# Matmuls on the identity ahead of TensorE's steps in the first job of a fused attention and mixture-of-experts kernel

## The chip, the cores and the metric

The kernel runs on one core of a Trainium2 chip. The metric is the device time of one execution in microseconds (us). The time before is 248.84 us, the median of three runs (248.19 to 251.78).

The engines are named as in the profile: PE is TensorE's matmul and PEld its weight load, DVE is VectorE, ACT is ScalarE, POOL is GpSimd, SP is SyncE, which issues the transfers here.

## The reference: what is computed

Attention with a sliding window and sink positions, over 4 batches, 8 heads, 768 positions and 64 columns per head, and on its output a soft mixture of 8 experts with 4 slots each. All is float32.

```python
scores = scale * np.matmul(q, k.transpose(0, 1, 3, 2))
keep = is_sink | in_window            # first 4 positions, or the last 128 up to the own one
a = exp(scores - max) / (sum + 1e-09) # where keep, else 0
x = (a @ v) in rows of 512, one per token

logits = x @ phi                      # 32 slots
d = softmax of logits over the tokens;  slot_input = d.T @ x
slot_out[e] = relu(slot_input[e] @ w1[e]) @ w2[e]
out = softmax of logits over the slots @ slot_out
```

## The kernel before, in words

The attention is cut into 12 jobs (line 690): a job is one batch b and 256 query positions j. A job loads q, k and v of its positions (load, line 712), transposes k and q (prep, 729), makes four tiles of scores and their softmax (softmax, 765: two quads of heads, each with the even and the odd 64 rows of every block of 128), transposes the weights of a quad (weights_transposed, 841) and the weights of the sink positions (sinks_transposed, 851), masks the transposed weights (select, 863) and multiplies with v (values, 875). Then the tokens go through the gate of the mixture (Moe.tokens, 307). After the twelfth job the experts' weights, two matrices of 16 MB together 32 transfers of 1 MB, are multiplied (Moe.tail, 511). In the first job, prep works in two halves, and the four sink rows of v are split into a high and a low part (sink_values, 74).

No loop sets the order of the work. Each piece is a step with an engine, an estimated time, what it reads and writes, and a key (Plan.add, 161). Plan.order (167) runs a list schedule over all steps with these estimates: it takes the step that could start first, and the smallest key among those. Plan.issue (251) then writes the instructions in the order of the planned starts, each engine's queue being in order. At a TensorE step it takes the step's bank or banks of PSUM (lines 258 to 260): "s" is the pool of two score tiles of two banks each, "w" the pool of four single banks for all the rest. A new tile's first writer waits until the last reader of the tile that had the bank before has finished.

The kernel has matmuls on the identity already: 8 before the plan starts (line 1158), 10 steps of 128 columns that the plan puts where TensorE is free at the start (busy, line 925, with a key of 1000), and up to 64 of 64 columns in the last job (line 964). Nothing reads what they write.

The names in the profile: first is the buffer of loaded q and k, wt any of a pool of large slots (the transposed k, the weights, v, the experts' weights), qt the transposed q, s and w the PSUM tiles, pst and vsink the transposed sink weights and the sink rows of v, ident the identity. All instructions that the plan issues have line 127, that of the helper which records them.

Of the kernel before, what the change touches and what calls it, by code (L numbers as in the profile page):

```python
# [19 lines left out]
P = 128  # L20
# [96 lines left out]
class Engine:  # L117


    def __init__(self, tc, engine):  # L120
        self.tc, self.engine = tc, engine
# [19 lines left out]
class Plan:  # L141
# [8 lines left out]

    IDLE = 900.0

    def __init__(self, pools):

        self.pools, self.steps, self.modes, self.handles = pools, [], [], 0
# [95 lines left out]
    def issue(self):  # L251
        order = sorted(self.order())
        end = max(t for t, _, i, e in order if e == "P" and self.steps[i][0] < self.IDLE)
        for t, _, i, e in order:
            _, _, _, fn, _, _, new, _ = self.steps[i]
            if t > end and self.steps[i][0] >= self.IDLE:
                continue
            for x in new:
                pool, shape, _ = self.pools[x["kind"]]
                x["tile"] = pool.tile(shape, F32, name=x["kind"])  # L260
            fn(e)


# [384 lines left out]
def window_path(ctx, tc, c, moe, q, k, v, phi, w1, w2, out):  # L648
# [6 lines left out]
    nc = moe.nc = Core(tc)  # L655
    B, H, S, D = q.shape
    NJ = S // 256
    plan = Plan(moe.pools)
# [5 lines left out]
    def slot():  # L664
        return slots.tile([P, 2048], F32, name="wt")

    t, u = moe.first
# [7 lines left out]
    t = slot()  # L675
# [3 lines left out]
    t = slot()  # L679
# [245 lines left out]
    def busy(e, h, n=P):  # L925
        nc.tensor.matmul(h["tile"][:, 0:n], lhsT=c.ident, rhs=c.ident[:, 0:n], start=True, stop=True)


    for _ in range(WARM[1]):
        h = plan.psum()  # L930
# [196 lines left out]
def fused(ctx, tc, q, k, v, n_sink, window, phi, w1, w2, out):  # L1127
# [42 lines left out]
    with tc.If(flag == 1) as cmp:  # L1170
        with ExitStack() as c2:
            window_rest(tc, moe, *window_path(c2, tc, c, moe, q, k, v, phi, w1, w2, out), out)
# [33 lines left out]
```

## Time and profile before

| | |
|---|---|
| median of three runs | 248.84 us |
| profiled execution | 248.67 us |
| its span (first to last instruction) | 247.0 us |
| mean granted clock of TensorE | 0.971 |
| busy share of PE, DVE, ACT, POOL | 87%, 65%, 61%, 57% |
| mean DMA rate over the span | 241 GB/s |
| instructions | 8602, of them 3356 matmuls on PE |

How to read it: the profile's slices cut the span into 40 equal parts and give busy time in tenths, the clock that TensorE was granted in tenths of full speed, and the share of the 16 DMA engines in use. The chain is the work that ended last, followed back from the end. In the timeline a row is a group of like instructions, with the start in us from the span's begin, the time, and in brackets the engine's idle time ahead of it and what ended it. In a table of windows stand the window, its length, the busy time of PE, PEld, DVE, ACT and POOL with their instructions in brackets, the granted clock, the DMA share and GB/s.

### The profile page before, as it was taken

How to read it: one execution, taken by the hardware profiler on the slowest of the kernel's cores; microseconds unless marked ns; L12 is line 12 of the kernel's file. 1: busy time of each engine (PE TensorE's matmuls, PEld its weight loads, DVE VectorE, ACT ScalarE, POOL GpSimd, SP SyncE). 2: the span in 40 equal slices, each digit the busy share in tenths (PEclk: the TensorE clock that was granted, in tenths of full speed). 3: DMA queues.
4: the chain of work that ended last, by engine and by line, in shares of the span. 5: the costliest groups of instructions: out<-in, count | busy, mean ns of one | idle time of the engine just before them, and what ended most of it. 6: DMA issues, size and time to landing. Idle time of an engine off the chain costs nothing.

```text
span 247.0 us, 8602 instructions
## 1 busy us (share of the span) xinstructions
PE 214.8 (87%) x3356; PEld 152.0 (62%) x3356; DVE 161.3 (65%) x440; ACT 151.1 (61%) x577; POOL 141.9 (57%) x281
## 2 busy tenths in 40 slices
PE   7953899898999799999979899997999999999820
PEld 7733566576777567776747677664787534556520
DVE  4289568759899956889994888997544611225340
ACT  2167569869778886968888686888643411214320
POOL 2036687976857995885789497678995141000000
PEclk9996799999999999999999999999999999999985
DMA  5597989999899799999999999460149989999896
GB/s 117 114 199 157 169 255 280 257 268 287 240 213 285 239 284 262 281 251 205 265 202 245 242 335 198 91 215 1 31 160 330 372 333 344 348 349 367 315 319 204
DMA packets 102963, 59.44 MB, mean 241 GB/s; under 512 B 76292, under 2 KB 98820, under 8 KB 102916
## 3 DMA queue, kind: packets, MB, share of 16 engines
q1 hardware_dynamic: 102916, 58.83, 86.0%
q8 instruction: 28, 0.46, 0.8%
q14 instruction: 19, 0.16, 0.2%
HBM read 52.53 MB, written 6.29 MB: 238 GB/s over the span
## 4 chain that ended last, share of the span: by engine, by line
PE 51%; DVE 28%; ACT 13%; issue 4%; POOL 0%; ACTq 0%; DVEq 0%; POOLq 0%
PE w L127 34%; PE s L127 15%; DVE wt L127 13%; ACT wt L127 9%; DVE s L127 9%; DVE rs L127 2%; PE w L1158 2%; DVE first L127 1%; ACT wt L582 1%; ACT first L127 1%; DVE call L127 1%; DVE acc L127 1%; DVE sums L127 0%; DVE wt L567 0%; DVE vsink L127 0%
## 5 line engine op out<-in xcount | busy, mean ns | idle before, releaser
L127 ACT ACTIVATE wt<-s,wt 128x132 f32<-128x132 f32 x192 | 68.5, 376 | 10.7 <-DVE wt L127 4.5
L127 POOL TENSOR_TENSOR wt<-wt 128x528 f32<-128x528 f32 x96 | 63.8, 670 | 19.4 <-DVE wt L127 8.2
L127 POOL TENSOR_SCALAR_AFFINE_SELECT wt<-wt 128x512 f32<-128x512 f32 x88 | 54.4, 640 | 15.6 <-DVE sums L127 9.8
L127 PE MATMUL w<-wt 128*64 128x128 f32 (+3 forms) x550 | 50.7, 317 | 1.6 <-DVE wt L567 1.0
L127 PE MATMUL s<-wt,qt 64*64 64x196 f32 (+2 forms) x768 | 43.1, 332 | 10.0 <-ACT wt L127 7.0
L127 PEld LDWEIGHTS w<-wt 128*64 128x64 f32 (+2 forms) x550 | 35.9, 140 | 13.8 <-DVE wt L567 2.1
L127 ACT ACTIVATION_READ_ACCUMULATOR wt<-s,wt 128x1 f32 x192 | 40.5, 211 | 0.0
L127 PEld LDWEIGHTS s<-wt,qt 64*64 64x64 f32 x768 | 27.0, 136 | 20.1 <-ACT wt L127 10.5
L127 DVE TENSOR_REDUCE wt<-s 128x4 f32<-128x528 f32 x48 | 33.9, 707 | 1.7
L127 PE MATMUL w<-ident,wt 64*128 64x64 f32 (+1 forms) x442 | 28.9, 239 | 3.7 <-POOL wt L127 1.2
L127 ACT COPY wt<-w 128x512 f32<-128x512 f32 (+1 forms) x41 | 23.7, 581 | 11.7 <-PE w L127 8.6
L127 PEld LDWEIGHTS w<-ident,wt 64*128 64x128 f32 (+1 forms) x442 | 21.2, 142 | 13.2 <-issue 6.6
L127 DVE COPY wt<-w 128x512 f32<-128x512 f32 (+1 forms) x33 | 22.0, 666 | 10.8 <-PE w L127 10.8
L127 PEld LDWEIGHTS w<-ident,first 64*128 64x128 f32 x576 | 21.8, 141 | 10.7 <-issue 5.0
L127 PE MATMUL w<-ident,first 64*128 64x64 f32 x576 | 26.9, 231 | 1.5 <-ACT first L127 1.5
L127 ACT COPY first<-w 128x512 f32<-128x512 f32 x32 | 18.6, 592 | 15.5 <-PE w L127 15.4
L127 DVE COPY_PREDICATED s<-later,s 128x256 f32<-128x256 uint8 x48 | 20.4, 425 | 4.4 <-PE s L127 3.2
L127 DVE TENSOR_TENSOR wt<-wt 128x4 f32<-128x4 f32 x48 | 13.6, 283 | 10.2 <-ACT wt L127 9.0
L127 ACT ACTIVATE qt<-w 128x512 f32<-128x512 f32 (+1 forms) x25 | 14.4, 579 | 6.2 <-PE w L127 4.3
L127 PE MATMUL s<-wt 128*32 128x256 f32 x256 | 14.4, 380 | 0.0
L127 PE MATMUL w<-wt,si 128*32 128x512 f32 x112 | 14.1, 594 | 0.0
L127 POOL COPY wt<-wt 128x512 f32<-128x512 f32 (+2 forms) x13 | 5.7, 455 | 13.5 <-ACT wt L127 11.0
(115 smaller groups left out, 246.1 us busy)
## 6 DMA issues: line engine op xcount, KB each, us to landing
wt<-in_moe_w_dram SPq DMA_DIRECT2D x30, 1024.0 KB, 8.2
wt<-in_v_dram SPq DMA_DIRECT2D x24, 256.0 KB, 4.5
first<-in_q_dram SPq DMA_DIRECT2D x22, 256.0 KB, 5.5
first<-in_k_dram SPq DMA_DIRECT2D x22, 256.0 KB, 4.6
out_dram<-wt SPq DMA_DIRECT2D x4, 1024.0 KB, 7.6
first<-in_moe_w_dram SPq DMA_DIRECT2D x2, 1024.0 KB, 5.1
out_dram<-wt SPq DMA_DIRECT2D x3, 512.0 KB
first<-in_k_dram SPq DMA_DIRECT2D x4, 128.0 KB, 2.3
```

The lines of the kernel that those rows point to most:

```text
L127: return self.tc.keep_in_program_order(f(*args, **kw))
L582: (nc.vector.tensor_copy if n % 2 else nc.scalar.copy)(ob[:, 2 * (n - n0):2 * (n - n0) + 2], yp)
L1158: nc.tensor.matmul(t[:, 0:P], lhsT=c.ident, rhs=c.ident, start=True, stop=True)
```

## The change

Plan.issue gets a variable, free, the planned end of the last TensorE step. When a TensorE step is planned to start later than that, and its planned start is below 30 us, the gap divided by 0.11 us gives a number of matmuls, which are issued right ahead of the step into the step's own (first) bank. Each multiplies the 128x128 identity with 64 of its columns. The step's own first matmul starts a new accumulation and overwrites what they wrote. The order of the steps stays the same, and the other engines' instructions do too.

```diff
+    FILL = 30.0
...
     def issue(self):
         order = sorted(self.order())
         end = max(t for t, _, i, e in order if e == "P" and self.steps[i][0] < self.IDLE)
+        free = None
         for t, _, i, e in order:
...
             for x in new:
                 pool, shape, _ = self.pools[x["kind"]]
                 x["tile"] = pool.tile(shape, F32, name=x["kind"])
+            if e == "P":
+                if free is not None and t < self.FILL:
+
+                    for _ in range(int((t - free) / 0.11)):
+                        self.fill(new[0]["tile"])
+                free = t + self.steps[i][2][0]
             fn(e)
...
+    def fill(t):
+        nc.tensor.matmul(t[:, 0:64] if len(t.shape) == 2 else t[:, 0, 0:64], lhsT=c.ident, rhs=c.ident[:, 0:64],
+                         start=True, stop=True, skip_group_check=True)
+
+    plan.fill = fill
```

99 such matmuls are issued, called fills below, ahead of 16 steps: 1, 1 and 3 among the first transposes and identity matmuls, 8 ahead of the first scores, 1 ahead of the second half of the transposes, 19 ahead of the sink rows' matmul, 1 and 3 ahead of the first job's other scores, 2 ahead of the second job's transposes of q, 19 ahead of the first transposes of weights, 3 ahead of the second job's transposes of k, 20 ahead of its scores, 1 ahead of the next transposes, 15 ahead of the sink transposes, 1 ahead of the next scores and 1 ahead of the first values. Three of these places follow, as the instructions stand on TensorE; the brackets are the semaphores that an instruction waits for.

The sink rows' matmul (w<-wt 128x256), behind the transposes of q and k of the first job. Before:

```order
L127 MATMUL w<-ident,first_76 128x64 [waits DMAHW0_49]
L127 MATMUL w<-ident,first_76 128x64 x3
L127 MATMUL w<-wt 128x256 [waits DMAHW6_49,DMAHW5_49,DMAHW7_49,DMAHW4_49,Activation_49]
L127 MATMUL s<-wt,qt 64x68 [waits DVE_49,Activation_49,Pool_49]
L127 MATMUL s<-wt,qt 64x196 [waits DVE_49]
```

Now:

```order
L127 MATMUL w<-ident,first_76 128x64 [waits DMAHW0_49]
L127 MATMUL w<-ident,first_76 128x64 x3
L127 MATMUL w<-ident 128x64 [waits Activation_49]
L127 MATMUL w<-ident 128x64 x18
L127 MATMUL w<-wt 128x256 [waits DMAHW6_49,DMAHW7_49,DMAHW5_49,DMAHW4_49]
L127 MATMUL s<-ident 128x64 [waits DVE_49,Activation_49]
L127 MATMUL s<-wt,qt 64x68 [waits Pool_49]
L127 MATMUL s<-wt,qt 64x196 [waits DVE_49]
```

The wait for ScalarE, which frees the bank, has gone from the step to the first of its 19 fills.

The second job's first scores (s<-wt,qt 64x196), behind its transposes of k. Before:

```order
L127 MATMUL w<-ident,first_76 128x64 [waits DMAHW3_49]
L127 MATMUL w<-ident,first_76 128x64 x7
L127 MATMUL s<-wt,qt 64x196 [waits DVE_49]
L127 MATMUL s<-wt,qt 64x196 [waits Activation_49]
L127 MATMUL s<-wt,qt 64x196 x14
```

Now:

```order
L127 MATMUL w<-ident,first_76 128x64 [waits DMAHW3_49]
L127 MATMUL w<-ident,first_76 128x64 x7
L127 MATMUL s<-ident 128x64 x20
L127 MATMUL s<-wt,qt 64x196 [waits DVE_49]
L127 MATMUL s<-wt,qt 64x196 [waits Activation_49]
L127 MATMUL s<-wt,qt 64x196 x14
```

Here the 20 fills wait for nothing, and the step still waits for VectorE, which copies the transposed k.

The sink transposes (w<-ident,wt 128x128), behind the second transposes of weights (w<-ident,wt 128x64). Before:

```order
L127 MATMUL w<-ident,wt 128x64 [waits Pool_49]
L127 MATMUL w<-ident,wt 128x64 x7
L127 MATMUL w<-ident,wt 128x128 [waits Activation_49]
L127 MATMUL w<-ident,wt 128x128 [waits Pool_49]
L127 MATMUL s<-wt,qt 64x196 [waits DVE_49]
```

Now:

```order
L127 MATMUL w<-ident,wt 128x64 [waits Pool_49]
L127 MATMUL w<-ident,wt 128x64 x7
L127 MATMUL w<-ident 128x64 [waits Activation_49]
L127 MATMUL w<-ident 128x64 x14
L127 MATMUL w<-ident,wt 128x128
L127 MATMUL w<-ident,wt 128x128 [waits Pool_49]
L127 MATMUL s<-ident 128x64 [waits DVE_49]
```

Again the wait for ScalarE, for the bank, has gone from the step to the first of 15 fills.

## The prediction

> **What bounds the kernel now.** I read the page first: the span, the slices of busy time and the chain that ended last.
>
> ```profile
> span 247.0 us, 8602 instructions
> ...
> PE   7953899898999799999979899997999999999820
> ...
> PEclk9996799999999999999999999999999999999985
> DMA  5597989999899799999999999460149989999896
> ...
> PE w L127 34%; PE s L127 15%; DVE wt L127 13%; ACT wt L127 9%; DVE s L127 9%; DVE rs L127 2%; PE w L1158 2%; DVE first L127 1%; ACT wt L582 1%; ACT first L127 1%; DVE call L127 1%; DVE acc L127 1%; DVE sums L127 0%; DVE wt L567 0%; DVE vsink L127 0%
> ```
>
> A slice is 6.2 us. TensorE is at 9 or 8 in nearly all of them and holds half of the chain (51% in the page's sum by engine). It is idle mainly in the first five slices, the ones that the change fills, and the fourth and fifth are the only ones before the very end in which its granted clock is below full. The windows place that dip:
>
> ```profile
> 20.00:22.00 2.00, 1.29 (x23) 1.27 (x24) 1.85 (x7) 1.85 (x8) 1.12 (x3) 0.71 0.79 174
> 22.00:24.00 2.00, 0.37 (x7) 0.18 (x3) 2.00 (x4) 1.37 (x8) 1.84 (x2) 0.50 0.33 75
> 26.00:28.00 2.00, 2.00 (x30) 1.20 (x24) 1.17 (x3) 0.00 (x0) 1.38 (x4) 0.58 1.23 209
> 28.00:30.00 2.00, 1.04 (x32) 0.90 (x30) 1.93 (x5) 1.98 (x10) 0.16 (x1) 1.00 0.20 46
> ```
>
> The third number from the right is the granted clock: half speed from inside the first of these windows to the end of the third, some 6.8 us. Now the same stretch as TensorE's own timeline; a bracket is the idle time ahead of a group and what ended it.
>
> ```profile
> 9.03 0.59 PE L127 MATMUL w<-ident,first 64*128 64x64 f32 x8
> 10.18 1.56 PE L127 MATMUL s<-wt,qt 64*64 64x68 f32 x32 [0.57 <-ACT qt L127]
> 11.67 0.71 PE L127 MATMUL w<-ident,first 64*128 64x64 f32 x16
> 12.60 0.69 PE L127 MATMUL w<-wt 32*128 32x256 f32 x2 [0.22 <-ACT qt L127]
> 15.23 0.30 PE L127 MATMUL s<-wt,qt 64*64 64x68 f32 x2 [1.94 <-ACT wt L127]
> 15.85 1.77 PE L127 MATMUL s<-wt,qt 64*64 64x196 f32 x30 [0.32 <-DVE wt L127]
> 17.55 0.71 PE L127 MATMUL w<-ident,first 64*128 64x64 f32 x16
> 19.01 0.46 PE L127 MATMUL w<-ident,wt 64*128 64x64 f32 x7 [0.69 <-ACT qt L127]
> 20.71 0.61 PE L127 MATMUL w<-ident,wt 64*128 64x64 f32 x8 [1.24 <-POOL wt L127]
> 21.12 1.25 PE L127 MATMUL w<-ident,first 64*128 64x64 f32 x16
> 24.43 3.47 PE L127 MATMUL s<-wt,qt 64*64 64x196 f32 x32 [2.06 <-DVE wt L127]
> 27.83 0.71 PE L127 MATMUL w<-ident,first 64*128 64x64 f32 x16
> 28.38 0.67 PE L127 MATMUL w<-ident,wt 64*128 64x64 f32 x16
> 30.07 0.44 PE L127 MATMUL w<-ident,wt 128*128 128x128 f32 x2 [1.03 <-ACT wt L127]
> 30.44 0.89 PE L127 MATMUL s<-wt,qt 64*64 64x196 f32 x16
> 31.26 0.50 PE L127 MATMUL w<-pst,vsink 128*128 128x256 f32 x2
> ```
>
> The brackets add up to 0.57 + 0.22 + 1.94 + 0.32 + 0.69 + 1.24 + 2.06 + 1.03 = 8.1 us of idle time, all that there is to fill. The half clock shows in two rows: 16 transposes take 1.25 us at 21.12 where their like takes 0.71, and 32 score instructions take 3.47 us at 24.43 where 16 take 0.89 at full clock. So it costs 0.54 + (3.47 - 2 x 0.89) = 2.2 us. That is the whole prize.
>
> **The price of one fill.** The order of the changed kernel puts 99 matmuls on the identity between these steps. The trace of before has the same instruction late in the program (128x64, float32, on the identity, into a score bank). Narrow windows there give starts of successive ones:
>
> ```profile
> 177.52 0.39 PE L127 MATMUL s<-ident 128*128 128x64 f32 x2
> 177.63 0.43 PE L127 MATMUL s<-ident 128*128 128x64 f32 x2
> L127 PEld LDWEIGHTS s<-ident x34: 186/190/198, 177.2 to 193.9; 128*128 128x128 f32 x34
> ```
>
> Starts are 0.11 us apart at full clock. But one matmul of the program is two such instructions, each with its own weight load: the 16 score matmuls of two steps stand as x32 in the timeline above. A fill therefore holds TensorE for 0.22 us, twice the 0.11 by which the planner divides a gap into fills, and 99 of them for 21.8 us: 8.1 us of idle time cannot hold that. The bounds are 0.11 (the two halves overlap wholly) and 0.28 (one and a half weight loads of 190 ns, if they didn't overlap well); 0.22 is nearest to the rows.
>
> The Trainium skill, "TensorE: Matmul & The Clock Gate", section "Back-to-back issue gap", gives N/2.4 + 2.5 ns for a matmul on its own at full clock, 29 ns for 64 columns, so an estimated 0.06 us for a fill of two; by that the fills would fit into the gaps and the time would stay at about 249. Its section "LDWEIGHTS" charges columns/1.2, an estimated 107 ns for 128 columns, which is what the rows show. The trace agrees with the second: the weight load sets the pace here.
>
> **Step by step.** Fills stand in TensorE's in-order queue ahead of their step and need only the step's bank. So the lateness of a step grows by its fills and shrinks by the idle time that it had; the other engines' inputs to it come from TensorE's earlier steps, which are late by less, so that they are there in time unless said otherwise.
>
> 1. One, one and three fills ahead of the first transposes, eight ahead of the first scores: 13 x 0.22 = 2.86, less the 0.57 idle: 2.3 us late (the copy of q is late by the first five fills alone, 1.1).
> 2. One fill ahead of the transposes at 11.67: 2.5.
> 3. 19 fills ahead of the sink rows' matmul at 12.60. Its bank comes free with the copy of q that ended the 0.22 idle; this copy is itself 2.5 late, so nothing of the fills is hidden: 2.5 + 4.18 = 6.7. This is the first place where a fill waits for the bank and then delays the step that waited for it too.
> 4. One ahead of the scores at 15.23, less 1.94 + 0.32: 4.65. Three ahead of the next scores: 5.3. Two ahead of the transposes at 17.55: 5.75.
> 5. 19 ahead of the transposes of the weights, less 0.69 + 1.24: 8.0. The weights themselves, GpSimd's product that ended the wait at 20.71, are at most 4.65 late, like the scores. Three more: 8.65.
> 6. The transposes at 21.12 now run at full clock: 8.1. 20 fills ahead of the scores at 24.43, less 2.06: 10.45. The scores at full clock, 1.7 less: 8.8. One fill: 9.0 for the transposes at 27.83 and 28.38.
> 7. 15 fills ahead of the sink transposes at 30.07. These wait for a bank, too:
>
> ```profile
> 26.73 0.43 DVE L127 COPY_PREDICATED s<-later,s 128x256 f32<-128x256 uint8 x1 [2.08 <-PE s L127]
> 28.02 0.37 ACT L127 ACTIVATE wt<-s,wt 128x132 f32<-128x132 f32 x1 [2.97 <-PE s L127]
> 29.42 0.60 ACT L127 COPY wt<-w 128x512 f32<-128x512 f32 x1
> ```
>
> ScalarE's copy at 29.42 frees it, behind four exponentials at 28.02 that need the mask at 26.73, which needs the first scores of step 6. These now start at 24.43 + 10.45 = 34.9 and take 0.89, so the mask starts at 35.85 and the bank is free 30.02 - 26.73 = 3.3 us behind it, at 39.15: 9.1 late, with no idle time left to hide the fills. 15 x 0.22 = 3.3 more: 12.4 late.
> 8. One ahead of the scores at 30.44, one ahead of the values at 31.26: 12.9.
>
> Each of the five stretches of idle time that I subtracted (0.57, 1.94 + 0.32, 0.69, 1.24, 2.06) is some 0.1 us larger than its bracket says, since a group's modelled end overlaps the next start (11.67 starts before 10.18 + 1.56 has ended). That takes back 0.5: **12.4 us late** where the fills end.
>
> **What becomes of it.** From 30.07 on the order holds the same instructions as before. The lateness reaches the end if no engine had a backlog that TensorE can now catch up with, and if the transfers of the last stage don't start by a clock of their own.
>
> ```profile
> 36.61 0.59 ACT L127 COPY first<-w 128x512 f32<-128x512 f32 x1 [1.23 <-PE w L127]
> 37.28 0.69 DVE L127 COPY wt<-w 128x512 f32<-128x512 f32 x1 [1.10 <-PE w L127]
> 40.00:44.00 4.00, 3.46 (x65) 2.16 (x55) 3.74 (x11) 3.46 (x16) 3.10 (x6) 1.00 0.97 298
> 44.00:50.00 6.00, 5.48 (x86) 3.89 (x86) 3.92 (x12) 4.81 (x19) 5.83 (x13) 1.00 0.90 254
> 50.00:60.00 10.00, 9.24 (x173) 7.16 (x173) 7.48 (x21) 7.82 (x35) 6.52 (x13) 1.00 0.96 278
> 170.00:175.00 5.00, 4.43 (x67) 3.08 (x67) 3.29 (x11) 3.81 (x18) 4.71 (x11) 1.00 0.02 5
> 205.00:215.00 10.00, 10.00 (x125) 5.14 (x118) 1.56 (x6) 1.65 (x6) 0.00 (x0) 1.00 1.07 345
> ```
>
> ScalarE and VectorE both wait for TensorE at 36.6 and 37.3, so by then they had no backlog. The DMA share is 0.02 at 170 to 175 and over 1 at 205: the queue stands still until the attention's slots come free, then runs full, so the tail starts when the attention ends and moves with it. I pass on all of the 12.4.
>
> The profiled execution took 248.67 us for a span of 247.0, 1.67 around it, 0.17 under the median of 248.84. 247.0 + 12.4 + 1.67 = 261.1 us, 4.9% over the median.
>
> **Rivals.** (a) *A fill is cheap.* At 0.11 a fill, the planner's price, the same steps read: 0.86 late at the first scores, 1.0 at 15.85 (the wait takes all of the 19), 1.7 at the weights' transposes, 1.6 at 24.43, nothing after the clock's 2.2, then 15 x 0.11 behind the late bank and two more: 2.1, less 0.5, 250.3 us. If also no fill lay behind a late bank, only the 2.2 would be left: 246.5. Not slower by 2%, then, as long as a fill takes under some 0.15 us (5.0 us late lies between 1.6 at 0.11 and 12.4 at 0.22). For it: the planner's number, and the instructions' halves overlap in part; against it: the starts 0.11 apart, two to a fill. It can't be faster by 2% (5 us): the idle time that was there is kept, filled or not, and the clock gives 2.2. The gap rule of the Trainium skill, above, lands in this case too.
>
> (b) *The lateness is given back later.* TensorE idles 0.54 + 0.52 + 0.76 = 1.8 us in the three windows from 40 to 60 above; if a backlog made these, and again as much in the later jobs, 3 to 7 us come back: about 255. Against it: the two waits at 37.
>
> (c) *A fill is dearer*, 0.25 or more, as when a load of 190 ns doesn't overlap well, or the gate drops to half clock in the wait for the late bank of step 7: 99 x 0.03 = 3 us, 264.
>
> **How the numbers follow.** The forecast has 0.78, (a) 0.07, (b) 0.07, (c) 0.08. The range of 255 to 265 takes in (c) and the smaller half of what (b) gives back; (a) and the rest of (b) stay out. About 2%, 5 us, is what can be told from no change here. Slower by that is the forecast, (c) and most of (b): 0.91; within it (a) and a little of (b): 0.07; faster, against the bound of 2.2 us: 0.02.
>
> **What would show it.** A granted clock of 1.00 throughout the first 40 us; fills 0.11 us apart by instruction and two to a matmul; the sink rows' matmul at about 19.3, the first scores of the second job (24.43) at about 34 to 35, the sink transposes (30.07) at about 42, the values (31.26) at about 43.5; and the same distance of some 12 us between the two traces at the last row of the attention and at the end. I am wrong if the fills are closer than 0.11 to one another, if the distance at 31.26 is under 8 us, or if it shrinks on the way to the end.

## The result, and the profile after

The changed kernel takes 266.04 us (median of four runs, 265.89 to 266.65) against 249.18: 1.0688 times the time before, 95% interval 1.0639 to 1.0737. The direction, the price of a fill and the lateness up to the sink transposes were as forecast. What came behind them was not: 261.1 us was 5 us too little, and the time lies 1 us above the range. In what follows, ratios and their intervals leave out executions over 1.5% longer than the fastest of their kernel, while medians and ranges take in all. The page of the profiled execution (265.89 us):

```profile
span 264.2 us, 8992 instructions
...
PE   7999989998989997989998989998899999999840
...
PEclk9999995799999999999999999999999999999995
```

The early idle time of TensorE has gone from the slices, and the dip of the clock has not: it has moved from the fourth and fifth slice (6.2 us each) to the seventh and eighth (6.6 us each). The windows show it; the third number from the right is the granted clock, the first behind the comma is TensorE's busy time:

```profile
32.90:36.32 3.42, 3.42 (x51) 2.99 (x49) 0.68 (x2) 0.00 (x0) 0.71 (x3) 1.00 1.03 190
36.32:39.73 3.41, 2.18 (x41) 1.98 (x41) 2.44 (x6) 2.84 (x15) 1.21 (x2) 1.00 0.50 114
39.73:43.14 3.41, 3.41 (x18) 3.41 (x18) 0.00 (x0) 0.57 (x4) 1.07 (x2) 0.50 1.05 316
43.14:46.56 3.42, 3.42 (x25) 3.12 (x28) 0.42 (x1) 0.00 (x0) 1.05 (x3) 0.50 0.09 37
46.56:49.97 3.41, 3.41 (x22) 2.12 (x16) 1.38 (x4) 2.04 (x9) 1.06 (x1) 0.50 0.02 5
```

Half clock lasts 10.2 us instead of 6.8, and TensorE is busy all that time. TensorE's timeline at the places of the prediction's steps:

```profile
11.70 1.56 PE L127 MATMUL s<-wt,qt 64*64 64x68 f32 x32
...
14.48 4.46 PE L127 MATMUL w<-ident 128*128 128x64 f32 x38 [0.22 <-ACT qt L127]
18.87 0.69 PE L127 MATMUL w<-wt 32*128 32x256 f32 x2
...
23.55 4.46 PE L127 MATMUL w<-ident 128*128 128x64 f32 x38
27.93 0.72 PE L127 MATMUL w<-ident,wt 64*128 64x64 f32 x16
...
30.04 4.68 PE L127 MATMUL s<-ident 128*128 128x64 f32 x40
34.64 1.56 PE L127 MATMUL s<-wt,qt 64*64 64x196 f32 x32
...
38.94 5.97 PE L127 MATMUL w<-ident 128*128 128x64 f32 x30 [1.23 <-ACT wt L127]
44.70 0.64 PE L127 MATMUL w<-ident,wt 128*128 128x128 f32 x2
45.12 0.53 PE L127 MATMUL s<-ident 128*128 128x64 f32 x2
45.58 1.59 PE L127 MATMUL s<-wt,qt 64*64 64x196 f32 x16
47.10 0.69 PE L127 MATMUL w<-ident 128*128 128x64 f32 x2
47.54 0.77 PE L127 MATMUL w<-pst,vsink 128*128 128x256 f32 x2
48.25 2.35 PE L127 MATMUL w<-wt 128*64 128x256 f32 x16
50.52 0.89 PE L127 MATMUL s<-wt,qt 64*64 64x196 f32 x16
...
200.30 1.96 PE L127 MATMUL w<-wt 128*64 128x256 f32 x24
```

Two rows of the kernel before, for the distance:

```profile
33.14 0.89 PE L127 MATMUL s<-wt,qt 64*64 64x196 f32 x16
...
182.96 1.96 PE L127 MATMUL w<-wt 128*64 128x256 f32 x24
```

A fill is two instructions (19 stand as x38) and takes (18.87 - 14.48) / 19 = 0.23 us. The sink rows' matmul, forecast for 19.3, starts at 18.87; the second job's scores, forecast for 34.9, at 34.64; the bank of the sink transposes, forecast for 39.15, is free at 38.94. These three are right to 0.5 us. The first scores are not: forecast 2.3 us late, they start at 11.70 against 10.18, 1.5 us late. Then the 15 fills take 44.70 - 38.94 = 5.76 us in place of 3.3. The scores that stood at 33.14 before start at 50.52, 17.4 us late, and this distance stays nearly the same: the attention's last values start at 200.30 against 182.96, 17.3 us later, and the span is 17.2 us longer.

### The profile page after: what moved, and what is told of

Read it like the earlier page. It is cut to its first block, busy times and chain, and to the rows that moved or that the text cites. A ratio compares the mean times of both kernels' runs of the same rounds, so it can differ in the third digit from the quotient of the medians.

```text
span 264.2 us, 8992 instructions
## 1 busy us (share of the span) xinstructions
PE 238.9 (90%) x3554; PEld 176.7 (67%) x3554; DVE 160.9 (61%) x440; ACT 151.2 (57%) x577; POOL 142.1 (54%) x281
## 4 chain that ended last, share of the span: by engine, by line
PE 59%; DVE 22%; ACT 11%; issue 3%; POOL 0%; ACTq 0%; DVEq 0%; POOLq 0%
PE w L127 40%; PE s L127 18%; DVE wt L127 11%; ACT wt L127 9%; DVE s L127 7%; DVE rs L127 2%; PE w L1172 1%; DVE first L127 1%; ACT wt L591 1%; DVE call L127 1%; ACT first L127 1%; DVE acc L127 1%; DVE sums L127 0%; DVE wt L576 0%; ACT pst L127 0%
## 5 line engine op out<-in xcount | busy, mean ns | idle before, releaser
L127 PE MATMUL w<-wt 128*64 128x128 f32 (+3 forms) x550 | 51.5, 321 | 1.4 <-DVE wt L576 1.0
L127 PE MATMUL s<-wt,qt 64*64 64x196 f32 (+2 forms) x768 | 41.6, 328 | 5.1 <-ACT wt L127 5.1
L127 PEld LDWEIGHTS s<-wt,qt 64*64 64x64 f32 x768 | 26.1, 134 | 13.6 <-ACT wt L127 9.6
L127 PEld LDWEIGHTS w<-ident,first 64*128 64x128 f32 x576 | 21.1, 139 | 9.8 <-issue 4.2
L127 PE MATMUL w<-ident,first 64*128 64x64 f32 x576 | 26.2, 229 | 1.5 <-ACT first L127 1.5
L127 PE MATMUL w<-ident 128*128 128x64 f32 (+1 forms) x152 | 22.0, 305 | 1.4 <-ACT wt L127 1.2
L127 PEld LDWEIGHTS w<-ident 128*128 128x128 f32 x152 | 20.7, 217 | 3.4 <-issue 1.4
```

The costliest lines, as they stand in the source:

```text
L127: return self.tc.keep_in_program_order(f(*args, **kw))
```

## What the experiments had to tell apart

Why did the clock fall, and why did it take three stretches full of matmuls to come back? In all traces it changes on a grid of stretches of 3.41 us, counted from the first record of full clock (before: 13.65 = 4 x 3.41 us of full clock from 7.2 to 20.86, then 6.83 = 2 x 3.41 of half clock). Three theories:

- **A: what counts is the time in which columns stream through the array**, that is, in which TensorE multiplies and doesn't only load weights. A 256-column instruction takes (52.42 - 51.99) / 2 = 0.215 us in these two rows of the changed kernel, 0.84 ns per column:

```profile
51.99 0.50 PE L127 MATMUL w<-pst,vsink 128*128 128x256 f32 x2
52.42 1.52 PE L127 MATMUL w<-wt 128*64 128x256 f32 x16
```

  An instruction of a fill so streams for an estimated 54 of the 115 ns from one start to the next: under half of the time, however dense the fills are. With 128 columns it would stream for 108 ns and, if the weight load sets the pace, cost no more.
- **B: what counts is idle time**, and the 1.23 us of waiting for the bank brought the clock down.
- **C: the gate has a long memory**, and 30 us of half-streaming fills wore it down.

For A I worked out, from the traces' rows, the share of each 3.41 us stretch in which at least one instruction streams (columns x 0.84 ns from its start, twice that at half clock). These are estimates; they stand in a table behind the experiments.

## The experiments

All compute the whole output. Each is compared with the kernel before, run beside it on the same chip.

**The 15 fills ahead of the sink transposes with 128 columns.**

```diff
-                        self.fill(new[0]["tile"])
+                        self.fill(new[0]["tile"], 128 if k == 15 else 64)
```

> The 15 fills ahead of the sink transposes take 128 columns in place of 64, all else as in the change. Theory A (the clock gate counts the time in which columns stream; a fill of 64 columns streams for half of its time, two times 53 of 223 ns, one of 128 columns for nearly all of it): the stretch from 36.3 to 39.7 us, which streamed for an estimated 0.38 of its time and was followed by half clock, gets to about 0.50, above the 0.44 to 0.46 of stretches that kept the clock. So the clock stays at 1.00, or comes back after one stretch of 3.4 us; the 15 cost 3.3 us in place of 5.8, the steps behind them 2.3 us less: 261 us. Theory B (the gate counts idle time of the queue; 1.2 us of waiting for the bank did it): the wait is the same, the clock falls at the same place and stays for 10.2 us: 266 us.

Measured: 260.99 us (260.79 to 262.56), 1.0489 [1.0430, 1.0548]. TensorE's timeline, then the windows of that stretch:

```profile
38.49 3.62 PE L127 MATMUL w<-ident 128*128 128x128 f32 x30 [1.23 <-ACT wt L127]
41.95 0.38 PE L127 MATMUL w<-ident,wt 128*128 128x128 f32 x2
```

```profile
35.40:38.81 3.41, 2.18 (x48) 1.70 (x37) 2.88 (x7) 2.36 (x12) 0.73 (x2) 1.00 0.34 76
38.81:42.22 3.41, 3.41 (x33) 3.41 (x32) 0.00 (x0) 1.05 (x6) 1.55 (x2) 1.00 1.11 320
```

The wait for the bank is the same 1.23 us and the window as busy (2.18 us), yet the clock stays; the 15 fills, twice as wide, take 41.95 - 38.49 = 3.46 us in place of 5.76. Five of the 17 us were the half clock. This speaks against B. It is not quite the test I meant: here the grid lies so that the stretch ends at 38.81, with only 0.3 us of the wide fills in it. For a fair comparison the grid has to lie alike, and in the profile of the changed kernel's second series, below, it does.

**The other 84 with 128 columns.**

```diff
+                        self.fill(new[0]["tile"], 64 if k == 15 else 128)
```

> The other 84 fills take 128 columns, the 15 ahead of the sink transposes stay at 64. A fill of 128 columns starts every 0.22 us at full clock like one of 64 columns, so no time is added by that. Theory A (streaming time, stretch by stretch of 3.4 us): the stretch ahead of the drop holds only one of the 84, so the clock falls as in the change and the time is 266 us. Theory C (the gate has a long memory: 30 us of fills at half their time had worn it down): the clock stays, 261 us.

Measured: 261.99 us, 1.0496 [1.0431, 1.0560]; its four runs are 261.43, 261.94, 262.05 and 266.41, and the last is not in the ratio. My expectation from A, that the clock falls and the time is 266, was wrong for three of the four, and at first sight C has it. The stretch with the wait, in the profiled run (262.05):

```profile
37.13:40.55 3.42, 2.25 (x44) 1.99 (x40) 2.64 (x6) 2.69 (x14) 1.01 (x2) 1.00 0.43 95
```

It streams for an estimated 0.41, in the changed kernel for 0.38; one of the 84 wide fills lies in it, and the grid lies otherwise. In the run at 266.41 the mean granted clock was 0.973, in the others 0.984 to 0.988: with the same instructions, the clock fell in one run and not in three. What differs from run to run in the traces is the place of the grid; that it decides here is likely but not shown.

**The changed kernel once more.**

> The changed kernel once more, to see how its runs spread. Theory A (streaming time, in stretches of 3.4 us whose place against the program differs from run to run): the stretch that holds the wait for the bank sits at the edge (0.38 where it fell, 0.41 to 0.42 in three variants where it did not), so most runs are at 266 us and some may be at 261 to 262. Theory B (the idle time decides): all are at 266 us.

Measured: 260.60, 265.39, 266.32, 266.54, 266.63 and 266.87 us. One run in six is 5 us faster than the rest with the very same instructions, as A at its edge allows. B and C have no room for that. Of this run there is no trace, but its mean granted clock is on record: 0.983, as with the 15 wide ones (0.983 to 0.986), against 0.964 to 0.970 in the other five. So its clock stayed up.

The profiled run (265.39 us) is the partner that the 15 wide fills lacked:

```profile
35.48:38.90 3.42, 2.19 (x45) 1.74 (x38) 2.85 (x7) 2.41 (x12) 0.77 (x2) 1.00 0.33 73
38.90:42.31 3.41, 3.41 (x18) 3.41 (x18) 0.00 (x0) 1.01 (x6) 1.50 (x2) 0.50 1.12 316
```

```profile
38.54 6.37 PE L127 MATMUL w<-ident 128*128 128x64 f32 x30 [1.23 <-ACT wt L127]
```

Here the stretch ends 38.90 - 38.54 = 0.36 us behind the start of the 15 fills, with the wide ones 38.81 - 38.49 = 0.32. The wait (1.23 us), the busy time (2.19 and 2.18 us) and the DMA share (0.33 and 0.34) are alike; the width of the fills differs, and the chip. The clock falls with 64 columns and stays with 128. One trace of each is little, and the estimated streaming is close, 0.39 against 0.41; but it goes the way of A, and B is out.

**The 15 left out.**

```diff
+                        if k != 15: self.fill(new[0]["tile"])
```

> The 15 fills ahead of the sink transposes are left out, 84 stay. Those 15 and the two behind them hold TensorE from 38.9 to 47.5 us in the trace of the change. Theory A: the bank comes free 8.9 us later than before, one fill each ahead of the scores and the values make it 9.3, the steps behind the bank stream well, and the clock stays or falls for one stretch of 3.4 us at most (1.7 us): 258.5 us, up to 260. Theory B (idle time): the wait for the bank of 1.2 us still brings half clock for 10 us over steps that cost 5 us at full clock: 263 us or more.

Measured: 257.56 us (257.38 to 258.66), 1.0343 [1.0288, 1.0397].

```profile
38.85 0.44 PE L127 MATMUL w<-ident,wt 128*128 128x128 f32 x2 [1.23 <-ACT wt L127]
```

```profile
36.12:39.53 3.41, 2.18 (x42) 1.90 (x46) 2.75 (x7) 2.73 (x14) 1.09 (x2) 1.00 0.44 101
39.53:42.94 3.41, 3.41 (x52) 2.40 (x50) 2.32 (x6) 2.59 (x12) 2.95 (x6) 1.00 1.09 339
```

The same 1.23 us of waiting, and the clock stays at 1.00 (0.42 streaming, and streaming steps behind it). B, which had 263 us or more, fails here too; A's 258.5 was 0.9 us too much. Against the 15 wide fills it is 3.4 us faster, the whole cost of 15 fills behind a late bank; against the change 8.5 us.

**All 99 with 128 columns.**

```diff
-        nc.tensor.matmul(t[:, 0:64] if len(t.shape) == 2 else t[:, 0, 0:64], lhsT=c.ident, rhs=c.ident[:, 0:64],
+        nc.tensor.matmul(t[:, 0:128] if len(t.shape) == 2 else t[:, 0, 0:128], lhsT=c.ident, rhs=c.ident[:, 0:128],
```

> All 99 fills take 128 columns. A fill starts every 0.22 to 0.23 us at full clock, as with 64 columns. Theory A: every stretch of fills streams for over 0.8 of its time, and even if the clock fell in the wait for the bank, the next stretch would bring it back; 261 to 262 us in every run, about 5 us less than the change for the same number of fills. Theory B: 266 us.

Measured: 262.58 us (261.75 to 263.09, six runs), 1.0558 [1.0527, 1.0588]. Twice the columns, and 3.5 us less than the change, not quite the 5 expected; every run is far from 266. The prediction's 261.1 is within 1.5 us of this kernel, which has the fills but not the half clock.

**Half as many: the divisor 0.22, 43 fills of 64 columns.**

```diff
-                    for _ in range(int((t - free) / 0.11)):
+                    k = int((t - free) / 0.22)
+                    for _ in range(k):
```

> A gap is divided by 0.22 us, what a fill takes, in place of 0.11: 43 fills in place of 99. Theory A by the sums of the prediction: 0.5 us late at the first scores, 0.5 at the second quad's, 1.0 at the transposes of weights, 0.9 at the second job's scores, minus 0.8 behind them at full clock, then 7 fills behind the late bank, 1.6: 0.6 to 1.1 us late, 250 us, with a clock of 1.00 throughout. Rival: fewer fills stream too little, the clock falls around 20 us as before, nothing is regained, and the lateness is 3 us: 252 us.

Measured: 253.11 us, 1.0133 [1.0083, 1.0182]. A's 250 us with the clock up was wrong, and the rival's 252 us with a fallen clock came nearer. The profiled execution is the slowest of its five (257.86; the others 252.3 to 253.4), so it is the worst case. Its mean granted clock was 0.943. The others had 0.969 to 0.974, which is still less than the 0.982 to 0.989 of the three kernels above whose clock stayed up to the end in their profiles (the 15 wide, the 15 left out, all 99 wide), so their clock seems to have fallen as well, for a shorter time. The profile shows the trap at its plainest:

```profile
11.58:14.99 3.41, 3.19 (x28) 2.60 (x24) 3.22 (x11) 2.86 (x14) 0.20 (x1) 1.00 0.79 167
14.99:18.40 3.41, 3.26 (x32) 2.32 (x32) 1.73 (x7) 1.33 (x8) 2.14 (x4) 0.50 1.32 214
21.82:25.23 3.41, 3.41 (x26) 3.29 (x27) 0.34 (x2) 1.38 (x7) 1.07 (x1) 0.50 0.64 139
28.64:32.06 3.42, 3.42 (x19) 3.29 (x22) 0.18 (x1) 0.18 (x1) 2.06 (x4) 0.50 1.27 244
32.06:35.47 3.41, 3.41 (x48) 2.39 (x42) 1.87 (x4) 0.79 (x5) 0.00 (x0) 0.50 0.22 36
```

The clock falls behind a stretch with 0.22 us of idle time and stays at half for 20.5 us, in most of which TensorE is busy without a gap. It comes back behind the first one that is full of scores (32.06). Fills of 64 columns left the clock where it was: up in the change to 39.73 us, down here once it had fallen. And it fell 10 us after it had come up, so that no 30 us of wear are needed: C explains nothing here that A does not.

**The same 43 with 128 columns.**

> 43 fills (the divisor 0.22) with 128 columns. The 43 with 64 columns took 253 us, and their profile shows half clock from 15 to 35 us, through stretches that are full of fills and stream for 0.50 to 0.60. Theory A: those stretches would now stream for 0.8 or more, so the clock stays or comes back at once: the sums of the prediction at this number give 250 us. If something else than streaming keeps it down: 253 us again.

Measured: 249.96 us (248.96 to 251.42, ten runs), 1.0069 [1.0041, 1.0096], as the sums say. Its windows:

```profile
13.93:17.35 3.42, 3.33 (x33) 2.37 (x32) 2.61 (x11) 3.10 (x17) 0.86 (x3) 1.00 1.17 229
20.76:24.17 3.41, 3.41 (x50) 3.03 (x49) 3.25 (x8) 3.12 (x15) 2.38 (x5) 1.00 0.68 151
```

**Only 18, of 128 columns, where idle time holds them.**

```diff
+                    k = int((t - free) / 0.11)
+                    for _ in range(9 if k == 20 or k == 19 and len(new) == 2 else 0):
```

> Only 18 fills, of 128 columns: nine ahead of the transposes of weights (the idle 0.69 and 1.24 us, with the bank free and the step's second half waiting for GpSimd) and nine ahead of the second job's first scores (idle 2.06 us); none ahead of a step whose bank comes late. 9 x 0.22 = 2.0 us fits into both. By the prediction's accounting no step is later, and the clock stays at 1.00 from 20.9 to 27.7 us: the scores take 1.7 us less, of which the copies behind them pass on 1.4: 247.5 us, up to 2.2 us under before. Rival: the first half of the weights' transposes is held up by the fills and takes VectorE or ScalarE along: no gain, 249 us or more.

Measured: 248.50 us (247.34 to 249.99, twelve runs), 1.0009 [0.9977, 1.0041]: no gain that can be told. The profiled run came out where the forecast had it (247.43 us), though it lost clock from 15.08 to 18.49 us, which the forecast did not have; so the number was met in part by luck:

```profile
11.66:15.08 3.42, 1.31 (x14) 0.83 (x16) 3.12 (x12) 2.87 (x16) 0.54 (x2) 1.00 0.77 168
15.08:18.49 3.41, 3.41 (x43) 2.40 (x38) 2.14 (x6) 0.76 (x6) 1.81 (x4) 0.50 1.17 211
20.86:24.28 3.42, 3.42 (x52) 3.08 (x46) 2.91 (x8) 2.66 (x11) 2.76 (x5) 1.00 0.66 140
```

The runs form two groups, six at 247.3 to 248.1 us and six at 248.9 to 250.0. Their mean granted clocks overlap (0.975 to 0.977 and 0.968 to 0.976), so what parts them is open.

**27: nine more ahead of the sink rows' matmul.**

```diff
+                    for _ in range(9 if k in (19, 20) else 0):
```

> 27 fills of 128 columns: the 18 of the run before and nine ahead of the sink rows' matmul. That step's bank comes late, so its nine fills, 2.0 us, delay it; but nothing waits for it within the next 2 us, and the scores behind it in the queue have 2.26 us of idle time. The 18 alone left half clock from 15.1 to 18.5 us in their profile, behind a stretch that streamed for 0.26 of its time, and runs at 247.3 to 248.1 as well as at 248.9 to 250.0 us. Theory A: that stretch streams for over 0.6 now, the clock stays, and the runs lie at 247 to 248 us, 1 us under before. Rival: the scores are late by the fills after all and the gain of 1.4 us is used up: 248.5 to 249 us.

Measured: 248.33 us (247.17 to 249.69, twelve runs) against 249.91 in the same comparison: 0.9950 [0.9915, 0.9985]. This is the only version whose interval lies below the kernel before, by 0.5%, in a comparison where the kernel before itself took 248.08 to 251.85. In the profiled run (247.99 us) the stretch that had lost the clock with 18 fills keeps it:

```profile
12.77:16.19 3.42, 3.33 (x36) 2.37 (x34) 2.56 (x11) 3.14 (x17) 0.88 (x2) 1.00 1.18 234
```

But the runs still spread over 2.5 us, so my "the runs lie at 247 to 248 us" was too much. The six up to 247.99 us had mean granted clocks of 0.982 to 0.987, the six from 248.67 on 0.975 to 0.980, so the clock seems to have stayed up in half of them.

The stretches in one table, with the estimated streaming:

| kernel | stretch, us | clock in it | TensorE busy | streaming | then |
|---|---|---|---|---|---|
| before | 14.03 to 17.44 | 1.00 | 0.56 | 0.46 | stays |
| before | 17.44 to 20.86 | 1.00 | 0.44 | 0.24 | falls |
| before | 24.27 to 27.68 | 0.50 | 0.95 | 0.93 | rises |
| change | 36.32 to 39.73 | 1.00 | 0.64 | 0.38 | falls |
| change | 39.73 to 43.14 | 0.50 | 1.00 | 0.50 | stays half |
| change | 43.14 to 46.56 | 0.50 | 1.00 | 0.68 | stays half |
| change | 46.56 to 49.97 | 0.50 | 1.00 | 0.88 | rises |
| change, again | 35.48 to 38.90 | 1.00 | 0.64 | 0.39 | falls |
| change, again | 45.72 to 49.13 | 0.50 | 1.00 | 0.87 | rises |
| 15 wide | 35.40 to 38.81 | 1.00 | 0.64 | 0.41 | stays |
| 84 wide | 37.13 to 40.55 | 1.00 | 0.66 | 0.41 | stays |
| 15 left out | 36.12 to 39.53 | 1.00 | 0.64 | 0.42 | stays |
| 43 of 64 | 11.58 to 14.99 | 1.00 | 0.94 | 0.44 | falls |
| 43 of 64 | 14.99 to 18.40 | 0.50 | 0.96 | 0.77 | stays half |
| 43 of 64 | 18.40 to 32.06, four | 0.50 | 1.00 | 0.52 to 0.60 | stays half |
| 43 of 64 | 32.06 to 35.47 | 0.50 | 1.00 | 0.94 | rises |
| 18 wide | 15.08 to 18.49 | 0.50 | 1.00 | 0.90 | rises |

Busy time sorts neither the falls (0.94 falls, 0.56 stays) nor the rises (1.00 stays half, 0.95 rises). Streaming sorts the rises cleanly, between 0.77 and 0.87, and the falls but for one row: 0.44 fell where 0.41 and 0.42 stayed. The rows of the table were picked; the same estimate for every whole stretch at full clock in the eleven traces, 764 of them, says the same. All 12 below 0.40 were followed by half clock, and of the 752 from 0.41 on, 748 were not. The four that were are the row with 0.44 and, at 0.44, 0.44 and 0.48, the last stretch with work at the end of three programs. So the lower edge is somewhere about 0.4, and what exactly the clock gate adds up there is open.

## Why the prediction was right and wrong

**Right: the price of a fill.** 0.22 by the late rows of before, 0.23 measured at full clock, not the planner's 0.11. Rival (a), the cheap fill, fails at its first condition.

**Right, but for step 1: steps 1 to 6 and the late bank.** Step 1 was 0.8 us off, it seems by the place of the grid. Four profiles with the same instructions up to the first scores started these at 11.25 us (the 15 wide), 11.30 (the change, again), 11.61 (the 15 left out) and 11.70 (the change) where the first full clock came at 4.68, 4.76, 5.40 and 5.60 us, about 0.5 us later for each us. In the profile of before it came at 7.21; by that slope, an estimate, the change would have started them at 12.5, the 2.3 us late of the forecast. The fills ahead of a step whose bank comes late start only there and are paid in full; leaving out the 15 shows it without the clock in the way (3.4 us between the two kernels at full clock).

**Right: nothing is given back.** 17.4 us at 50.5, 17.3 at 200.3, 17.2 at the end. Rival (b) is out.

**Wrong: step 7's "15 x 0.22 = 3.3 more", and step 8 behind it.** Both were priced at full clock; the forecast put the loss of clock behind the wait for the late bank at nothing. The clock fell to half at 39.73, 0.8 us into the 15 fills, and stayed there until 49.97. The 15 took 5.76 us, 2.5 more, and the stretch from the sink transposes (44.70, 14.63 late) to the scores at 50.52 (17.38 late) added 2.75 where its two fills should add 0.44: 2.3 more. Together 4.8 of the 5 us missed. Rival (c) had the place, "the gate drops to half clock in the wait for the late bank of step 7", but not the size: I priced it by dearer loads, 3 us, instead of by twice the time of all that stands behind the drop. With 261.1 + 4.8 = 265.9 it would have met the time. The experiments give the same split: 266.04 of the change against 260.99 where only the 15 are wider.

**Wrong beneath that: that fills count as full work for the clock.** Step 6 took for granted that fills keep the clock up, and my list of what would show the forecast had "A granted clock of 1.00 throughout the first 40 us". It held to 39.73, 0.3 us short of that, and told nothing of what came then. The Trainium skill, "TensorE: Matmul & The Clock Gate", section "What's actually happening", has full clock come back after one busy window of some 3.4 us. The grid of 3.41 us agrees; if busy means that TensorE has an instruction under way, the rule does not hold for this work. The change went through two fully busy stretches at half clock, the 43 fills through four and a nearly full one (0.96), and what brought the clock back each time was a stretch that streamed for 0.87 or more. The measurement decides.

## What to carry to other kernels

Price a filler by the row of the same instruction, count its weight loads, and never put it behind a wait that its step has anyway: there it hides nothing and is paid in full. If a filler is to keep the clock up, it must stream: here 128 columns cost at full clock what 64 do and made 3 to 5 us of difference (253.11 against 249.96 with 43 fills, 266.04 against 260.99 with 99), while stretches full of 64-column fillers did not bring a fallen clock back. And weigh the prize first: 2.2 us of half clock stood against 99 x 0.22 us of fills; the best placement found gained 0.5%.

## What the runs showed of the hardware

- The granted clock moves on a grid of 3.41 us that lies differently against the program in each run: the first full clock came at 4.68 to 7.41 us in these traces. The same instructions took 260.60 us at a mean granted clock of 0.983 and 265.39 to 266.87 at 0.964 to 0.970; that the place of the grid makes this difference is likely, not shown.
- Rise and fall have different edges in the estimated streaming: between 0.77 and 0.87 to rise, about 0.4 to fall, with four falls at 0.44 to 0.48. Between them the clock mostly stayed as it was, so a short dip can become a long one (20.5 us with 43 fills against 6.8 us with none).
- With a 128x128 float32 weight load to each instruction, 64 and 128 columns start equally far apart at full clock (0.116 us in a group of 19 narrow fills, 0.115 in the 15 wide ones, with two instructions to a fill). So the columns don't set the pace there; that the weight load does is inferred.
